# Order of the opening steps in a fused attention and feed-forward kernel: block 0's second queries and tile 0's values emitted ahead of the second key block's mixing and transposes, and one small key copy given to ScalarE

## The chip, the core and the metric

The kernel runs on one NeuronCore of one Trainium2 chip. The metric is the device time of one execution in microseconds (us), and a lower time is better. The kernel before ran five times: 209.24, 210.72, 212.59, 213.64 and 216.31 us, so the median is 212.59 us. The execution that the profile shows is the one of 209.24 us; its span from first to last instruction is 207.5 us, which leaves 1.74 us around the span.

Engines are named as in the profile: PE is TensorE (its matmuls), PEld its weight loads, DVE is VectorE, ACT is ScalarE, POOL is GpSimd, SP is the sync engine, whose queue issues DMAs. "L354" is line 354 of the kernel.

## What is computed

Attention over chunks with a memory, and then a feed-forward block with a residual. Inputs are float32; there are 4 batches, 8 heads, 768 positions, head size 64, and 8 memory keys and values per head.

```python
for c in range(S // 32):                       # chunks of 32 queries
    l, r = max(0, 32*c - 16), min(S, 32*c + 32 + 8)
    k_full = concat([mem_k, k[:, :, l:r]])     # 8 + up to 56 keys
    v_full = concat([mem_v, v[:, :, l:r]])
    a = softmax(q[:, :, 32*c:32*c+32] @ k_full.T / 8)
    out[:, :, 32*c:32*c+32] = a @ v_full
x = out with the heads side by side            # (4, 768, 512)
xn = (x - mean) / sqrt(var + 1e-6) * g_ln
result = x + relu(xn @ w_ch1) @ w_ch2          # 512 -> 2048 -> 512
```

## The kernel before

**Tiles.** A tile is 128 positions of one batch; a batch has six tiles, and three tiles make one of eight feed-forward units. Keys and queries arrive in blocks of 256 positions (two tiles). A block is first rearranged ("mixed") from the staging tile `st` or a raw float32 tile into `iv` (`mix`, L302; `mix_raw`, L268), then transposed on PE (`transpose_block`, L228; `half_q`, L290) into a PSUM bank, and copied from there into `KT` (keys: `window`, L218, with `key_piece`, L188) or `QR` (queries: `part_q`, L264). `KT` has groups of 64 positions; each holds its own keys, 16 keys to the left, 8 to the right, and the 8 memory keys. A tile reads two groups. Group 3, the second of tile 1, has as its right neighbours the first eight keys of block 1, and `first_right` (L212) copies them, four at a time, from the bank into which block 1 was transposed.

**One tile's way.** `scores` (L319, matmuls at L326) multiplies keys by queries into a pair of banks; `soften` (L335) takes the exponential on ACT, once for each half; `values` (L345: `weigh`, matmuls at L354, and `gather`, L361) multiplies by the values `V` and divides by the sum on DVE; `norm` (L374) subtracts the mean and multiplies by the gain, on DVE; `turn_x` (L395, L404, L409) transposes the result on PE and copies it; then `up_tile`, `up_two` and `up` multiply by the first weights, with a ReLU on ACT or DVE, and `down` and `paired` by the second. `v_mem` (L142) copies the memory values into `V`, two groups at a time here, on DVE. `spread_g` (L696, matmuls at L698) brings the gain vector `g_ln` onto all partitions in bank `mm[3]`; `norm(0, 0)` reads it there, and ACT copies it into `gb` for later tiles. `warm` (L591) is a matmul on zeros whose result nobody reads.

**What sets the order.** The schedule is written by hand. [...] From line 775 on, a table of steps (`at`) does the emitting for the steady part; the opening, lines 700 to 774, is a plain list of calls. The diff lies in lines 719 to 740 of that list. The DMAs of the opening are emitted before it, from line 605 to 690, and none lies among the lines of the diff.

**The queues around the diff, before.** On PE: `scores(0,0)`, eight transposes of the keys of block 1 into `mm[2]`, half of `spread_g`, the transposes of the second half of block 0's queries (into `att[1]`), `weigh(0,0)`, the other half of `spread_g`, `scores(0,1)`, four warm matmuls, `turn_x(0,0)`, `weigh(0,1)`, `up_tile(0,0,0)`. On DVE: `mix(0,1,0)`, two copies of `mix_raw`, `v_mem(0,0,2)`, `part_q`, the two copies of `first_right`, `gather(0,0)`, `norm(0,0)`, `v_mem(0,2,4)`. On ACT: `soften(0,0,0)`, `soften(0,0,1)`, four copies of `window` (pieces 2 and 3 of block 0), `soften(0,1,0)`, `soften(0,1,1)`, the copy of `gb`.

The second half of block 0's queries, which these lines transpose and copy, is what `scores(0,1)` reads; tile 0's own queries were copied before `scores(0,0)`.

Of the kernel before, what the change touches and what calls it, by code (L numbers as in the profile page):

```python
# [15 lines left out]
def kernel(  # L16
# [19 lines left out]
    W = 104  # L36
    GW = 4 * W
# [25 lines left out]
    KT = [t[:, 0 : NG * GW].rearrange("p (g j k) -> p g j k", g=NG, j=4) for t in KR]  # L63
# [20 lines left out]
    mm = [ps.tile([128, 512], FP32, name=f"mm{i}") for i in range(4)]  # L84
# [10 lines left out]
    def free(ap, off, pattern, parts=None):  # L95
        p = list(ap.ap[0]) if parts is None else [ap.ap[0][0], parts]
        return bass.AP(tensor=ap.tensor, offset=ap.offset + off, ap=[p] + [list(x) for x in pattern])

    def as16(t):
        return t.bitcast(FP16)  # L100

    def copy(eng, out, in_):
        if eng is nc.scalar:
            eng.copy(out=out, in_=in_)  # L104
        else:
            eng.tensor_copy(out=out, in_=in_)  # L106

    dve, act, pool = nc.vector, nc.scalar, nc.gpsimd
    ring = {}

    def pick(lst, key):
        key = (id(lst),) + key
        if key not in ring:
            ring[key] = ring.setdefault(("n", id(lst)), 0) % len(lst)
            ring[("n", id(lst))] += 1
        return lst[ring[key]]
# [25 lines left out]
    def v_mem(b, g0, g1, eng):  # L142
        src = memv16[96:W, b, :, :]
        copy(eng, free(V[b % 2][96:W, g0:g1, :, :], 0, [[H * VW, g1 - g0], [1, H * VW]]),
             bass.AP(tensor=src.tensor, offset=src.offset,
                     ap=[list(src.ap[0]), [0, g1 - g0], [1, H * VW]]))
# [41 lines left out]
    def key_piece(b, src, g, first, lo, n, eng, half=None):  # L188

        h, m = (0, 8) if half is None else (4 * half, 4)  # L190
        copy(eng, free(KT[b % 2], GW * g + 16 + 8 * lo + h, [[W, 4], [8, n], [1, m]]),
             free(src, 4 * (first + lo), [[1, 4], [4, n], [128, m]]))
# [16 lines left out]
            key_piece(b, banks[phase], 4 * blk + n, *PIECES[n], dve, phase)  # L209
            key_piece(b, banks[1 - phase], 4 * blk + 2 + n, *PIECES[2 + n], act, 1 - phase)  # L210

    def first_right(b, g, banks):  # L212

        for half in range(2):
            copy(dve, free(KT[b % 2], GW * g + 80 + 4 * half, [[W, 4], [1, 4]]),
                 free(banks[half], 0, [[1, 4], [128, 4]]))

    def window(b, blk, banks, k0, eng):  # L218

        for half in ((0, 1) if eng is dve else (1, 0)):  # L220
            key_piece(b, banks[half], 4 * blk + k0, *PIECES[k0], eng, half)
# [6 lines left out]
    def transpose_block(b, blk, which, banks):  # L228
        i = pick(iv, ("b", b, blk, which))
        for r in range(8):  # L230
            pv = banks[r // 4 if len(banks) == 2 else 0]
            c = 128 * (r % 4 if len(banks) == 2 else r)
            nc.tensor.matmul(  # L233
                out=pv[:, c : c + 128], lhsT=i[:, 128 * r : 128 * r + 128],
                rhs=order4 if which else identity,
                is_transpose=True, start=True, stop=True,
            )
# [26 lines left out]
    def part_q(b, blk, half, pv, eng):  # L264
        copy(eng, free(QR[b % 2], 1024 * blk + 64 * half, [[128, 8], [1, 64]]),
             free(pv, 64 * half, [[128, 8], [1, 64]]))

    def mix_raw(which, srcs, half, eng, lo=0, hi=128):  # L268

        o = pick(iv, ("b", 0, 0, which))[lo:hi, :]  # L270
        r0, n = (0, 8) if half is None else (4 * half, 4)
        for par in range(2):
            copy(eng, free(o, 128 * r0 + 64 * par, [[128, n], [1, 64]]),
                 free(srcs[par][lo:hi, :], 64 * r0, [[64, n], [1, 64]]))
# [15 lines left out]
    def half_q(b, blk, half, pv):  # L290

        i = pick(iv, ("b", b, blk, 1))
        rows = slice(64 * half, 64 * half + 64)
        for r in range(8):
            c = 128 * r + 64 * half
            nc.tensor.matmul(
                out=pv[:, c : c + 64],
                lhsT=i[rows, 128 * r : 128 * r + 128], rhs=order4[rows, rows],
                is_transpose=True, start=True, stop=True, tile_position=(64 * half, 0),
            )  # L300

    def mix(b, blk, which, eng):  # L302
        s, o = pick(st, ("b", b, blk, which)), pick(iv, ("b", b, blk, which))
        copy(eng, free(o, 0, [[64, 2], [128, 8], [1, 64]]), s)
# [14 lines left out]
    def scores(b, t):  # L319
        p = slot("att")  # L320
        score_slot[b, t] = p
        for gg in range(2):
            for j in range(4):
                for par in range(2):
                    rows = slice(64 * par, 64 * par + 64)
                    nc.tensor.matmul(  # L326
                        out=p[:, par, (4 * gg + j) * 64 : (4 * gg + j) * 64 + 64],
                        lhsT=free(KR[b % 2][rows, :], GW * (2 * t + gg) + W * j, [[1, 128]]),
                        rhs=free(QR[b % 2][rows, t // 2, :, :], 8 * gg +
                                 (32 * j + 16 * (t % 2) if (b, t) >= (1, 4) else 64 * (t % 2) + 16 * j),  # L330
                                 [[128, 8], [1, 8]]),
                        start=True, stop=True, tile_position=(64 * par, 0),
                    )

    def soften(b, t, c):  # L335
        p = score_slot[b, t]
        nc.scalar.activation(  # L337
            out=free(AT[t % 3], 32 * c, [[64, 16], [1, 32]]),
            in_=free(p, 4 * c, [[64, 16], [1, 4], [8, 8]], W),
            func=ACTF.Exp, bias=band[0:W, c : c + 1], scale=0.125,  # L340
        )
# [3 lines left out]
    def values(b, t):  # L345
        weigh(b, t)
        gather(b, t)

    def weigh(b, t):
        p = value_slot[b, t] = slot("att")  # L350
        for par in range(2):
            for j in range(4):
                for gg in range(2):
                    nc.tensor.matmul(  # L354
                        out=p[64 * gg : 64 * gg + 64, par, 128 * j : 128 * j + HD],
                        lhsT=AT[t % 3][:, par, gg, j, :],
                        rhs=V[b % 2][:, 2 * t + gg, 4 * par + j, 0:HD],
                        start=(j == 0), stop=(j == 3), tile_position=(0, 64 * gg),
                    )

    def gather(b, t):  # L361
        p, r, x = value_slot[b, t], rec[t % 2], xs[(NT * b + t) % 9]
        nc.vector.reciprocal(out=r, in_=free(p, 64, [[128, 8]]))
        nc.vector.scalar_tensor_tensor(  # L364
            out=x.rearrange("p (h d) -> p h d", h=8),
            in0=free(p, 0, [[128, 8], [1, 64]]), scalar=1.0,
            in1=free(r, 0, [[1, 8], [0, 64]]),
            op0=ALU.mult, op1=ALU.mult, accum_out=tot[t],
        )
        nc.vector.tensor_scalar(  # L370
            out=nmean[t], in0=tot[t], scalar1=-1.0 / 512, scalar2=None, op0=ALU.mult
        )

    def norm(b, t, gb=gb):  # L374
        i = NT * b + t
        nc.vector.scalar_tensor_tensor(  # L376
            out=xn[i % 4], in0=xs[i % 9], scalar=nmean[t], in1=gb, op0=ALU.add, op1=ALU.mult,
        )
# [212 lines left out]
    def warm(n, m=512, p=None):  # L591
        p = mm[3] if p is None else p
        for _ in range(n):
            nc.tensor.matmul(out=p[:, 0:m], lhsT=zero[:, 0:128], rhs=zero[:, 0:m], start=True, stop=True)
# [97 lines left out]
    K0 = [as16(mm[0]), as16(mm[1])]  # L692
    Q0 = [as16(mm[2]), as16(mm[3])]
    K1 = [as16(mm[2])[:, 512 * h : 512 * h + 512] for h in range(2)]

    def spread_g(half):  # L696
        cols = slice(256 * half, 256 * half + 256)
        nc.tensor.matmul(out=mm[3][:, cols], lhsT=gone, rhs=gpad[:, cols], start=True, stop=True)  # L698
# [20 lines left out]
    mem_vals()  # L719
    soften(0, 0, 0)  # L720
    soften(0, 0, 1)
    mix(0, 1, 0, dve)
    transpose_block(0, 1, 0, K1)
    mix_raw(1, raws[1], None, dve, 64, 128)
    spread_g(0)
    half_q(0, 0, 1, as16(att[1][:, 1, :]))
    v_mem(0, 0, 2, dve)
    part_q(0, 0, 1, as16(att[1][:, 1, :]), dve)
    first_right(0, 3, K1)
    turn["att"] = 1  # L730
    values(0, 0)
    spread_g(1)
    norm(0, 0, mm[3])
    v_mem(0, 2, 4, dve)
    window(0, 0, K0, 2, act)
    window(0, 0, K0, 3, act)
    scores(0, 1)
    soften(0, 1, 0)
    soften(0, 1, 1)
# [223 lines left out]
```

## Time and profile before

| view | value |
|---|---|
| median of five runs | 212.59 us (209.24 to 216.31) |
| the profiled execution | 209.24 us; span 207.5 us; mean granted PE clock 0.988 |
| PE busy | 198.7 us, 96% of the span |
| DVE, ACT, POOL busy | 162.6, 109.2, 109.5 us |
| DMA moved | 28.11 MB, mean 136 GB/s |
| chain that ended last, by engine | PE 75%, DVE 3%, ACT 2% |
| matmuls of the first weights, 128x384 (L430) | 464, 81.1 us |

The page divides the span into 40 equal slices of 5.19 us; a digit is the busy share in tenths, and the row PEclk gives the granted clock of PE in tenths. A line of the timeline gives the start and the duration in us, the engine, the source line, the operation, output and inputs, how many instructions were merged into the line, and in brackets how long the engine stood idle before it and what ended that. Ends of matmuls are modelled, so the distance from one group's start to the next one's is the better measure of what a group costs on PE. A row of the table by stretches gives, for each engine, the busy time and in brackets the number of instructions, then the granted clock, the DMA share and the rate.

### The profile page before, as it was taken

The page shows a single profiled execution, that of the slowest core. Times are in us where ns is not written, and L with a number is a line of the kernel's source. Part 1 is how long each engine was busy: PE and PEld are TensorE (multiplying, and loading weights), DVE is VectorE, ACT ScalarE, POOL GpSimd, SP SyncE. Part 2 cuts the span into 40 slices and gives each one's busy share as a digit, 9 for nine tenths or more (in the row PEclk, how much of TensorE's full clock was granted, in tenths as well). Part 3 has the DMA queues.
Part 4 walks back from the last instruction along what each step waited for, and adds up shares of the span by engine and source line. Part 5 has one row for each costly group of instructions (what it writes and reads, how often), then busy time and mean ns, then how long its engine had stood idle before and what let it go on. Part 6 is the DMA issues. An engine that isn't in the chain of part 4 may idle for free.

```text
span 207.5 us, 5280 instructions
## 1 busy us (share of the span) xinstructions
PE 198.7 (96%) x2042; PEld 135.4 (65%) x2042; DVE 162.6 (78%) x404; ACT 109.2 (53%) x236; POOL 109.5 (53%) x189
## 2 busy tenths in 40 slices
PE   7797999999999999999999999999999999999992
PEld 2365885547754477587667766686758765877581
DVE  5878746597989999997797999995897669565553
ACT  2575469638776076807791366537850676022300
POOL 7966687869699899954797982400040014000000
PEclk9789999999999999999999999999999999999998
DMA  5999999999999999999996999577022211220012
GB/s 161 190 187 193 206 198 187 207 129 239 166 146 141 182 194 123 154 166 249 198 166 150 128 181 125 114 164 156 17 36 76 101 30 26 78 101 0 0 54 101
DMA packets 74099, 28.11 MB, mean 136 GB/s; under 512 B 62169, under 2 KB 70105, under 8 KB 74074
## 3 DMA queue, kind: packets, MB, share of 16 engines
q0 software_dynamic: 46336, 14.71, 67.0%
q1 hardware_dynamic: 27594, 12.80, 28.0%
q8 instruction: 16, 0.26, 0.5%
q10 hardware_dynamic: 144, 0.26, 0.5%
q14 instruction: 9, 0.07, 0.1%
HBM read 30.28 MB, written 6.29 MB: 176 GB/s over the span
## 4 chain that ended last, share of the span: by engine, by line
PE 75%; DVE 3%; ACT 2%; issue 0%; DVEq 0%
PE mm L430 36%; PE mm L522 16%; PE mm L475 16%; PE att L354 3%; PE att L326 3%; ACT AT L337 1%; DVE osb L538 1%; DVE xs L364 1%; PE att L404 1%; PE att L233 0%; PE mm L233 0%; ACT rT L422 0%; ACT junk L381 0%; DVE xn L376 0%; DVE three L492 0%
## 5 line engine op out<-in xcount | busy, mean ns | idle before, releaser
L430 PE MATMUL mm<-xT,w1c 128*128 128x384 f16 x464 | 81.1, 327 | 0.0
L422 ACT ACTIVATE rT<-mm 128x384 f16<-128x384 f32 (+1 forms) x78 | 38.3, 498 | 52.7 <-PE mm L430 47.0
L430 PEld LDWEIGHTS <-w1c 128*128 128x128 f16 x464 | 51.0, 115 | 21.0
L475 PE MATMUL mm<-w2c,rT 128*128 128x512 f16 x192 | 44.4, 379 | 0.0
L137 POOL DMA_DIRECT2D V<-in_v_dram x48 | 38.4, 809 | 4.2 <-issue 2.8
L424 DVE TENSOR_SCALAR rT<-mm 128x384 f16<-128x384 f32 (+1 forms) x47 | 26.1, 559 | 14.7 <-PE mm L430 11.6
L337 ACT ACTIVATE AT<-att,band 104x512 f16<-104x512 f32 x48 | 31.0, 687 | 4.1 <-PE att L326 3.8
L387 POOL TENSOR_SCALAR veps<-sq 128x1 f32<-128x1 f32 x24 | 8.0, 334 | 43.9 <-ACT junk L381 21.9
L475 PEld LDWEIGHTS <-rT 128*128 128x128 f16 x192 | 18.2, 98 | 19.5
L381 ACT ACTIVATE junk<-xs,nmean 128x512 f16<-128x512 f32 x24 | 17.3, 720 | 4.3 <-issue 1.8
L522 PEld LDWEIGHTS <-SA 128*128 128x128 f16 x184 | 18.0, 98 | 2.1
L123 POOL DMA_DIRECT2D st<-in_q_dram x28 | 16.1, 585 | 3.6 <-DMA st<-in_q_dram 2.6
L364 DVE SCALAR_TENSOR_TENSOR xs<-att,rec 128x512 f32<-128x512 f32 x24 | 16.6, 691 | 0.8
L391 POOL TENSOR_TENSOR rstd<-veps,mhalf 128x1 f32<-128x1 f32 x24 | 16.1, 672 | 2.0
L376 DVE SCALAR_TENSOR_TENSOR xn<-xs,nmean,gb 128x512 f16<-128x512 f32 x23 | 16.6, 746 | 0.3
L522 PE MATMUL mm<-T,SA 128*128 128x256 f16 x144 | 16.7, 272 | 0.0
L522 PEld LDWEIGHTS <-rT 128*128 128x128 f16 x144 | 14.1, 98 | 3.1 <-issue 0.3
L104 ACT COPY KT<-rawk 128x352 f16<-128x352 f16 (+2 forms) x14 | 10.3, 785 | 6.5 <-DMA rawk<-iv 6.5
L129 POOL DMA_DIRECT2D st<-in_k_dram x22 | 12.9, 593 | 1.0 <-DMA w2c<-in_moe_w_ch_dram 1.0
L522 PE MATMUL mm<-w2c,rT 128*128 128x256 f16 x96 | 12.4, 272 | 0.0
L106 DVE COPY V<-memv 8x2560 f16<-8x2560 f16 (+1 forms) x14 | 11.0, 784 | 0.4
L354 PEld LDWEIGHTS <-AT 104*64 104x64 f16 x384 | 7.8, 111 | 5.3 <-issue 3.3
(107 smaller groups left out, 233.8 us busy)
## 6 DMA issues: line engine op xcount, KB each, us to landing
out_dram<-osb SPq DMA_DIRECT2D x23, 256.0 KB, 3.0
V<-in_v_dram POOLq DMA_DIRECT2D x40, 96.0 KB, 5.7
st<-in_k_dram POOLq DMA_DIRECT2D x22, 128.0 KB, 4.9
w1c<-in_moe_w_ch_dram POOLq DMA_DIRECT2D x4, 512.0 KB, 7.9
st<-in_q_dram POOLq DMA_DIRECT2D x32, 64.0 KB, 4.9
w2c<-in_moe_w_ch_dram POOLq DMA_DIRECT2D x4, 512.0 KB, 9.0
st<-in_q_dram POOLq DMA_DIRECT2D x6, 128.0 KB, 7.9
V<-in_v_dram POOLq DMA_DIRECT2D x8, 80.0 KB, 5.3
```

Of the source, the lines that this page charges most:

```text
L123: nc.gpsimd.dma_start(out=s[32 * j : 32 * j + 32, :], in_=dram(q, (b * H + j) * HS + blk * 256 * D, [[512, 32], [4 * HS, 2], [1, 512]]),)
L137: nc.gpsimd.dma_start(out=V[b % 2][lo:hi, g, :, 0:64], in_=dram(v, b * H * HS + (64 * g - 16 + lo) * D, [[64, hi - lo], [HS, H], [1, 64]]),)
L337: nc.scalar.activation(out=free(AT[t % 3], 32 * c, [[64, 16], [1, 32]]), in_=free(p, 4 * c, [[64, 16], [1, 4], [8, 8]], W), func=ACTF.Exp, ...
L364: nc.vector.scalar_tensor_tensor(out=x.rearrange("p (h d) -> p h d", h=8), in0=free(p, 0, [[128, 8], [1, 64]]), scalar=1.0, in1=free(r, 0, ...
L376: nc.vector.scalar_tensor_tensor(out=xn[i % 4], in0=xs[i % 9], scalar=nmean[t], in1=gb, op0=ALU.add, op1=ALU.mult,)
L381: nc.scalar.activation(out=junk, in_=xs[(NT * b + t) % 9], func=ACTF.Square, bias=nmean[t], scale=1.0, accum_out=sq[t],)
L391: nc.gpsimd.tensor_tensor(out=rstd[(NT * b + t) % 9], in0=veps[t % 3], in1=mhalf, op=ALU.pow)
L422: nc.scalar.activation(out=o, in_=p, func=ACTF.Relu)
L424: nc.vector.tensor_scalar(out=o, in0=p, scalar1=0.0, scalar2=None, op0=ALU.max)
L430: nc.tensor.matmul(out=p, lhsT=free(w1c[c][:, dt, :], i, [[4, 128]]), rhs=xT[u % 2][:, dt, 128 * lo : 128 * (lo + n)], start=(dt == 0), st ...
L475: nc.tensor.matmul(out=p, lhsT=rT[c][:, k_, 128 * i : 128 * i + 128], rhs=w2c[c][:, k_, :], start=(c == 0 and k_ == 0), stop=(c == 3 and k ...
L522: nc.tensor.matmul(out=p, lhsT=left(h)[:, k_, :], rhs=right(h)[:, k_, :], start=(h == 0 and k_ == 0), stop=(h == 1 and k_ == 3),)
```

## The change

Two things change. The order of the calls after `soften(0, 0, 1)` is another: `mix(0,1,0)` and the transposes of block 1's keys, which came first, come after the second half of block 0's queries; the transposes come after `values(0, 0)` as well. The `window` calls on ACT stand earlier in the list, but on ACT they still follow the same two `soften`s. One warm matmul into `mm[2]` is added between `half_q` and `values`. And `first_right` takes the engine as an argument, which is now ACT.

```diff
-    def first_right(b, g, banks):
+    def first_right(b, g, banks, eng):
 
         for half in range(2):
-            copy(dve, free(KT[b % 2], GW * g + 80 + 4 * half, [[W, 4], [1, 4]]),
+            copy(eng, free(KT[b % 2], GW * g + 80 + 4 * half, [[W, 4], [1, 4]]),
                  free(banks[half], 0, [[1, 4], [128, 4]]))
...
     mem_vals()
     soften(0, 0, 0)
     soften(0, 0, 1)
-    mix(0, 1, 0, dve)
-    transpose_block(0, 1, 0, K1)
     mix_raw(1, raws[1], None, dve, 64, 128)
     spread_g(0)
     half_q(0, 0, 1, as16(att[1][:, 1, :]))
     v_mem(0, 0, 2, dve)
+    warm(1, 512, mm[2])
     part_q(0, 0, 1, as16(att[1][:, 1, :]), dve)
-    first_right(0, 3, K1)
+    mix(0, 1, 0, dve)
     turn["att"] = 1
     values(0, 0)
+    window(0, 0, K0, 2, act)
+    window(0, 0, K0, 3, act)
+    transpose_block(0, 1, 0, K1)
+    first_right(0, 3, K1, act)
     spread_g(1)
     norm(0, 0, mm[3])
     v_mem(0, 2, 4, dve)
-    window(0, 0, K0, 2, act)
-    window(0, 0, K0, 3, act)
     scores(0, 1)
     soften(0, 1, 0)
     soften(0, 1, 1)
```

## The prediction, made before the changed kernel was run

> **What bounds the kernel now.** I read the page's first two parts, then the chain that ended last, then the timeline around the diff.
>
> ```profile
> PE 198.7 (96%) x2042; PEld 135.4 (65%) x2042; DVE 162.6 (78%) x404; ACT 109.2 (53%) x236; POOL 109.5 (53%) x189
> ...
> PEclk9789999999999999999999999999999999999998
> ```
>
> PE is nearly full, and its clock falls below full only in the opening. The chain in order of time starts at 37.80 us and is all PE from 43 us on:
>
> ```profile
> 37.80 0.70 ACT junk L381 x2
> ...
> 43.55 0.86 PE mm L475 x4
> ```
>
> So the diff, which lies between 9 and 16 us, counts only by how far it moves PE's hand-over into the full stretch. The chain doesn't reach back there; I walk it by hand in the timeline of all engines.
>
> ```profile
> 9.21 0.41 DVE L106 COPY iv<-st 128x1024 f16<-128x1024 f16 x1
> 9.66 0.49 DVE L106 CAST iv<-osb 64x512 f16<-64x512 f32 x1
> 9.77 0.61 PE L326 MATMUL att<-QR,KT 64*128 64x64 f16 x16
> 10.31 1.04 PE L233 MATMUL mm<-identity,iv 128*128 128x128 f16 x8
> 10.42 1.26 ACT L337 ACTIVATE AT<-att,band 104x512 f16<-104x512 f32 x2 [0.48 <-PE att L326]
> 11.14 0.83 PE L698 MATMUL mm<-xs,xs 128*128 128x256 f32 x2
> 11.90 0.40 PE L296 MATMUL att<-order,iv 64*128 64x64 f16 x8
> 12.23 0.44 PE L354 MATMUL att<-V,AT 104*64 104x65 f16 x16
> 12.34 0.42 DVE L106 COPY QR<-att 128x512 f16<-128x512 f16 x1 [1.19 <-PE att L296]
> 12.68 0.24 DVE L106 COPY KT<-mm 128x16 f16<-128x16 f16 x2
> 12.84 0.20 DVE L363 RECIPROCAL rec<-att 128x8 f32<-128x8 f32 x1
> 13.23 0.41 PE L326 MATMUL att<-QR,KT 64*128 64x64 f16 x16
> ```
>
> PE runs here without a gap: transposes of block 1's keys, gain, tile 1's queries, tile 0's values, tile 1's scores, each started by the one before. DVE waits 1.19 us for the queries. Then it is DVE's turn to be late:
>
> ```profile
> 14.85 0.49 DVE L106 COPY V<-memv 8x1280 f16<-8x1280 f16 x1
> 15.40 0.44 PE L354 MATMUL att<-V,AT 104*64 104x65 f16 x16
> 17.92 0.41 PE L326 MATMUL att<-QR,KT 64*128 64x64 f16 x16 [0.67 <-ACT QR L104]
> 20.04 1.08 PE L457 MATMUL mm<-xT,w1c 128*128 128x128 f16 x16 [0.52 <-DVE xT L409]
> ```
>
> Tile 1's values start at 15.40, 0.06 after the DVE copy of memory values ends (15.34), and 0.46 after the second exponential ended (13.68 + 1.26 = 14.94). So gather, norm and `v_mem(0,2,4)` on DVE set this hand-over, and ACT has 0.40 us of slack.
>
> The clock of PE by stretches:
>
> ```profile
> 8.00:9.00 1.00, 1.00 (x10) 0.56 (x9) 0.95 (x5) 0.70 (x3) 1.00 (x2) 0.54 2.17 153
> 10.00:11.00 1.00, 1.00 (x23) 0.91 (x16) 0.97 (x3) 0.58 (x1) 1.00 (x2) 0.50 1.14 190
> 11.00:12.00 1.00, 1.00 (x10) 0.67 (x8) 0.14 (x1) 1.00 (x5) 0.61 (x1) 0.76 1.18 182
> ```
>
> At half clock 0.54 means that 0.92 of that microsecond was slow, 0.76 that 0.48 was: PE ran at half speed from 8.08 to 11.48.
>
> [...] 11.48 - 8.08 = 3.40 us at 0.50. [...] scores at 17.92 wait 0.67 us for a query copy, and the warm matmuls behind them, which need nothing of it, start after, at 18.26. [...] For `first_right`'s 16 elements [...] ACT's copies into KT took 292 ns at 144 elements and 321 ns at 176, which extrapolates to 0.18. I take 0.18.
>
> **The change, part by part.** Distances between starts are used for PE.
>
> *Transposes leave the front.* They held PE from 10.31 to 11.14, 0.83 us at half clock. In their place the gain's first half starts at 10.31. Its second half, at full clock, takes 13.23 - 12.60 = 0.63; [...] So queries at 11.37, where 0.11 us of slow clock remains; the full-clock 0.33 (11.90 to 12.23) becomes 0.39: PE free at 11.76, results at about 11.83 instead of 12.30. `mix_raw` must be done: with `mix` gone from 9.21 its two copies take 9.21 to 10.03, and the raw queries, issued by 4.1 with 5.0 to landing, are there by 9.1. Cover is over a microsecond.
>
> *The added warm matmul*: 0.215, PE free at 11.97. It hides nothing else: values wait for the exponentials until 11.68 and for `v_mem` until 10.7, so it costs these 0.21 us. Values start at 11.97 instead of 12.23 and end at 12.41.
>
> *DVE*: `part_q` at 11.87 instead of 12.34 (0.47 earlier). `mix` now follows; a copy that large kept DVE 0.45 (9.21 to 9.66), and a query copy 0.34 (12.34 to 12.68): mix at 12.21, done 12.62. `first_right`, gone from here, had cost 0.16 (12.68 to 12.84). The reciprocal can start at 12.66 instead of 12.84: 0.47 - 0.45 + 0.16 = 0.18 earlier. Gather and norm behind it keep their 1.23 us: norm at 13.89 instead of 14.07, if the gain is there.
>
> *The new wait.* The transposes now wait on PE for `mix`: start 12.62 + 0.06 = 12.68, so PE stands 0.34 us (12.34 to 12.68). Queued behind: the gain's second half (norm waits for it), `scores(0,1)`, and the warm matmuls. At full clock eight transposes take 0.45 (the chain shows 0.45 for eight at 47.01). Gain at 13.13, results at 13.83, just ahead of norm's 13.89. `scores(0,1)` at 13.13 + 0.63 = 13.76 instead of 13.23: **0.53 later**. Bounds: 13.5 if mix slips in behind the queries sooner, 14.2 if half clock lasts longer.
>
> *`first_right` on ACT*: transposes end at 12.68 + 0.61 = 13.29; two copies end by 13.33 + 0.36 = 13.69. ACT is free since 12.47, the end of its `window` copies, whose place on ACT is the same. The copies are hidden under the gain's 0.63 by 0.07 us; without that cover each 0.1 us late makes scores 0.1 late.
>
> *The sum.* Exponentials 14.21 to 15.47 (1.26 us) instead of 14.94; tile 1's values at 15.47 + 0.05 = 15.52. DVE's side would be ready at 15.34 - 0.18 = 15.16. So DVE's delay is replaced by ACT's: 15.52 against 15.40, **+0.12 us**. Norm's output is turned after four warm matmuls, 13.76 + 0.34 + 0.86 = 14.96, against 14.88; its copy ends at 15.84 and `up_tile` starts at 15.97 against 15.85. ACT's queue behind (gain copy, two windows, each about 0.5 to 0.9 us) ends at 16.8, ahead of the query copy, which waits for PE (17.28 + 0.12). So scores of tile 2 and then `up_tile` at 20.04 are 0.12 later too.
>
> No DMA moves and neither SP's nor POOL's queue is touched; the second weights' third part, issued at 31.26 with 8.3 us to landing (39.6), is used at 40.34, so 0.12 us of delay costs no more there, and a gain over 0.7 us would be cut off. Profiled execution: span 207.5 + 0.12 = 207.62, time 209.24 + 0.12 = 209.36. The profiled run is the fastest of the five shown; their median is 212.59, so the forecast is **212.7 us**.
>
> **Rivals.**
>
> *The delay of `scores(0,1)` is smaller*: if it starts at 13.4, exponentials end at 15.11 and DVE's 15.16 decides: values at 15.22, 0.18 earlier than now, at most 0.3 if `mix` gains another tenth. 212.59 - 0.3 = 212.3 us. For it: PE's total work is unchanged, the transposes run at full clock. Against: `mix` sits behind `part_q`.
>
> *The clock is halved once more* (slower side). Place: PE between 14.9 and 18.3, where it is busy about 2.45 of 3.4 us, 72%, and keeps full clock; the 3.4 us ahead of the slow window were busy 1.99 us, 58%, and did not. The new wait at 12.34 and the later scores thin out PE in one of these windows. [...] 3.4 us at half clock cost 1.7: 214.4 us. Against: the new gap is 0.34 us, 10% of a window, in a stretch that was 92% busy.
>
> *Nothing moves, since another wait hides it*: PE waits for a part of the weights somewhere before 43 us, and the 0.12 is swallowed there. For it: that margin of 0.7 us; against: no wait for a DMA stands on PE in the profile. 212.6 us, not to be told from the forecast.
>
> **How the numbers follow.** Forecast, with the third rival in it (within 0.5 us of before): 0.72. Smaller delay, a gain of up to 0.3: 0.16. Clock or a longer ACT delay, 0.5 to 1.7 us slower: 0.12. All of these lie within 2%, 4.25 us, which is about what a measurement of this kernel can tell from no change. The scatter decides more than the edit: the middle three of the five runs lie from 210.72 to 213.64, and a new median may lie anywhere there. Range: 210.72 - 0.3 = 210.4 up to 213.64 + 1.7 = 215.3. That a median lies more than 2% off by scatter or a clock that I don't see I put at 0.06 faster and 0.08 slower.
>
> **What would show it.** Right: transposes (L233) after values at about 12.7 with PE idle before them for DVE's `iv`; `scores(0,1)` near 13.8; tile 1's values released by ACT's exponentials, not DVE's copy; `up_tile` near 16.0; the full stretch unchanged. Wrong: a second stretch at clock 0.5, values of tile 1 before 15.2, or PE waiting for `first_right`.

## The result, and the profile after

The change moves nothing that can be measured. Over 43 runs the changed kernel has a median of 210.17 us (208.39 to 217.8), over 80 runs beside it the kernel before has 211.5 us (208.32 to 217.85); the ratio of the times is 0.9994 with a 95% interval from 0.9974 to 1.0014. The medians lie further apart than the ratio says because they hold every execution, while the ratio leaves out those more than 1.5% above the fastest of their kernel, 13 of the 43 and 42 of the 80.

The forecast had the right direction (no change) and a level and a range that were too high: 212.7 us and 210.4 to 215.3, where 210.17 was measured. It also gave a wrong reason, which the new profile shows at once. Its execution took 210.93 us with a span of 209.1 us. First the page:

```profile
PE 198.3 (95%) x2043; PEld 134.7 (64%) x2043; DVE 163.0 (78%) x402; ACT 109.4 (52%) x238; POOL 108.3 (52%) x189
...
PEclk9999999999999999999999999999999999999999
```

This execution has no half clock in the opening (the granted clock is 1.00 in every stretch up to 45 us), so its moments can't be laid over those of before one to one. I count from the start of `scores(0,0)`, 9.77 us before and 8.78 here. The timeline of all engines:

```profile
8.78 0.41 PE L326 MATMUL att<-QR,KT 64*128 64x64 f16 x16 [0.22 <-DVE KT L106]
...
10.71 0.44 PE L354 MATMUL att<-V,AT 104*64 104x65 f16 x16
11.08 0.43 DVE L106 COPY iv<-st 128x1024 f16<-128x1024 f16 x1
...
11.56 0.62 PE L233 MATMUL mm<-identity,iv 128*128 128x128 f16 x8 [0.41 <-DVE iv L106]
...
12.22 0.25 ACT L104 COPY KT<-mm 128x16 f16<-128x16 f16 x2 [0.79 <-PE mm L233]
...
12.60 0.41 PE L326 MATMUL att<-QR,KT 64*128 64x64 f16 x16
...
13.05 1.26 ACT L337 ACTIVATE AT<-att,band 104x512 f16<-104x512 f32 x2 [0.59 <-PE att L326]
13.49 0.49 DVE L106 COPY V<-memv 8x1280 f16<-8x1280 f16 x1
...
15.24 0.19 PE L354 MATMUL att<-V,AT 104*64 104x65 f16 x1 [1.04 <-ACT KT L104]
...
15.83 0.42 PE L354 MATMUL att<-V,AT 104*64 104x65 f16 x15 [0.40 <-DMA V<-in_v_dram]
...
16.18 1.08 PE L457 MATMUL mm<-xT,w1c 128*128 128x128 f16 x16
```

The upper part is as forecast: the transposes wait 0.41 us for DVE's `mix`, the two small copies lie on ACT, and `scores(0,1)`, which stands behind the transposes on PE, comes later after `scores(0,0)` (3.82 us, not 3.46). Then comes what the forecast didn't have. The exponentials end at 14.31, DVE's copy of memory values at 13.98, and yet PE stands until 15.24, runs one matmul, and stands again until 15.83. Tile 1's values read `V` groups 2 and 3. These are the two loads of the changed kernel, with the time that they took from issue to landing (lowest, median, highest):

```profile
7.85 1.58 POOL L137 DMA_DIRECT2D V<-in_v_dram  x2
DMA to landing us min/median/max: 7.1/7.2/7.3
```

The first was issued at 7.85 and the second at about 8.64; they took 7.3 and 7.1 us, so they landed at about 15.15 and 15.75. The profile puts the first wait down to an ACT copy into `KT`, which tile 1's values don't read; the landing at 15.15 fits it, and the second wait is named as V. The same loads in the kernel before:

```profile
7.51 1.57 POOL L137 DMA_DIRECT2D V<-in_v_dram  x2
DMA to landing us min/median/max: 7.0/7.0/7.0
```

They were issued at 7.51 and 8.3, so they landed at 14.5 and 15.3. There PE started at 15.40, behind DVE's copy, which ended at 15.34: two possible releasers 0.04 us apart. The profile of before names no releaser at this row, so it can't say which of the two it was.

The two profiled spans differ by 1.6 us. 0.3 of it is there at `up_tile` (16.18 instead of 15.85), and still at 78 us (78.38 instead of 78.08 for one group of matmuls). The rest arises between 78 and 99 us, far behind the diff: there the chain now holds a transposing DMA of queries, which took 9.42 us.

```profile
82.51 9.42 DMA QR<-iv
...
93.26 0.75 DVE SA L492 x2
```

DVE waited 1.2 us for it, and PE 0.81 us for DVE after that. E6 below, in the old order, shows the same transposing DMA of 9.35 us with 0.7 us of waiting on PE, so it doesn't need the changed order.

### The profile page after: what moved, and what is told of

Its sections match the earlier page's. It is cut to its first block, busy times and chain, and to the rows that moved or that the text cites. A ratio compares the mean times of both kernels' runs of the same rounds, so it can differ in the third digit from the quotient of the medians.

```text
span 209.1 us, 5282 instructions
## 1 busy us (share of the span) xinstructions
PE 198.3 (95%) x2043; PEld 134.7 (64%) x2043; DVE 163.0 (78%) x402; ACT 109.4 (52%) x238; POOL 108.3 (52%) x189
## 4 chain that ended last, share of the span: by engine, by line
PE 67%; DVE 5%; DMA 5%; ACT 2%; issue 1%; DVEq 0%
PE mm L430 33%; PE mm L475 14%; PE mm L522 13%; DMA QR<-iv 5%; PE att L354 3%; DVE osb L538 3%; PE att L326 2%; ACT AT L337 1%; DVE xs L364 1%; PE att L404 1%; DVE three L492 0%; DVE KT L106 0%; PE att L233 0%; PE mm L233 0%; ACT rT L422 0%
## 5 line engine op out<-in xcount | busy, mean ns | idle before, releaser
L137 POOL DMA_DIRECT2D V<-in_v_dram x48 | 38.9, 819 | 5.0 <-DMA V<-in_v_dram 2.3
L387 POOL TENSOR_SCALAR veps<-sq 128x1 f32<-128x1 f32 x24 | 6.8, 284 | 43.9 <-ACT junk L381 21.9
L129 POOL DMA_DIRECT2D st<-in_k_dram x22 | 12.6, 584 | 1.7 <-DMA w2c<-in_moe_w_ch_dram 1.1
L106 DVE COPY iv<-st 128x1024 f16<-128x1024 f16 (+1 forms) x23 | 10.6, 463 | 1.5 <-DMA QR<-iv 1.2
```

Of the source, the lines that this page charges most:

```text
L137: nc.gpsimd.dma_start(out=V[b % 2][lo:hi, g, :, 0:64], in_=dram(v, b * H * HS + (64 * g - 16 + lo) * D, [[64, hi - lo], [HS, H], [1, 64]]),)
```

## The experiments

The theory after the result: the opening up to tile 1's values is closed by the landing of `V` groups 2 and 3; engines that are done earlier wait for it, whatever their order. The rival is the forecast's own reading: the queues of DVE and ACT close it.

**E1: the loads of V early, changed kernel.**

```diff
+    load_v(0, 2)
+    load_v(0, 3)
     load_w1(0)
     load_q(0, 1, 0)
-    load_v(0, 2)
-    load_v(0, 3)
     load_w1(1)
```

> The changed kernel with the loads of V groups 2 and 3 issued ahead of the first part of the first weights. Theory (the landing of V groups 2 and 3 releases tile 1's values in the changed kernel): the values of tile 1 start as soon as the exponentials are there, about 1.75 us after the start of scores(0,1), so near 14.4 us instead of 15.24 and 15.83, with no idle before them for a DMA; the first weights then land some 1.6 us later, near 15.4, and up_tile(0,0,0) starts near 15.4 instead of 16.18. Time 0.3 to 0.8 us below the changed kernel's, if nothing later takes it back. Rival (ACT's or DVE's queue releases the values, the DMA is only near): values stay at 15.2 or later, time as before.

Measured: 208.61 us (22 runs), 0.9913 of before, interval 0.9879 to 0.9947. Timeline of PE:

```profile
8.42 0.41 PE L326 MATMUL att<-QR,KT 64*128 64x64 f16 x16 [0.30 <-ACT QR L104]
...
13.58 0.44 PE L354 MATMUL att<-V,AT 104*64 104x65 f16 x16 [0.17 <-ACT AT L337]
...
13.95 1.08 PE L457 MATMUL mm<-xT,w1c 128*128 128x128 f16 x16
```

Tile 1's values now start when the exponentials are there, and `up_tile` comes 5.53 us after `scores(0,0)` instead of 7.40. The theory's reading holds. The first weights landed at about 13.9 us, 1.5 us sooner than expected, and `up_tile` did not wait for them. Between 0.9994 and 0.9913 lie 1.7 us, with some 0.8 us to either side by the two intervals; 0.3 to 0.8 us had been expected. I had cut the gain because of the margin of 0.7 us at the second weights; in this trace PE waits for no part of them.

**E2: the same loads early, kernel before.** The same edit.

> The kernel before with the same two loads moved ahead. Theory: DVE's copy of memory values stood at 15.34, 0.04 us after V group 3 landed (15.3), so without the DMA the values of tile 1 still start within 0.1 us of the end of that copy; the time is as before within 0.2 us. Rival (the DMA alone set the start in the kernel before as well): the values start up to 0.4 us earlier, when the exponentials end.

Measured: 209.16 us (22 runs), 0.9977 of before, interval 0.9943 to 1.0011. `up_tile` comes 5.87 us after `scores(0,0)`, 0.2 us less than before (6.08, with half clock in between).

```profile
13.92 0.49 DVE L106 COPY V<-memv 8x1280 f16<-8x1280 f16 x1
14.46 0.44 PE L354 MATMUL att<-V,AT 104*64 104x65 f16 x16
```

As the theory had it, tile 1's values start 0.05 us after the end of DVE's copy of memory values: with the load out of the way, DVE's queue is the last to be ready in the old order. The time can't be told from that of the kernel before.

**E3: no wait for V, changed kernel.** Tile 1's values read groups 0 and 1, so they wait neither for the loads of groups 2 and 3 nor for the second copy of memory values.

```diff
-                        rhs=V[b % 2][:, 2 * t + gg, 4 * par + j, 0:HD],
+                        rhs=V[b % 2][:, (0 if (b, t) == (0, 1) else 2 * t) + gg, 4 * par + j, 0:HD],
```

> The changed kernel in which tile 1's values read V groups 0 and 1 in place of 2 and 3, so that they wait for no load of V and for no memory value copy; tile 1's attention is then that of other values. Order and DMAs are untouched. Theory: values of tile 1 start 1.75 us after the start of scores(0,1), about 14.4 us, up_tile(0,0,0) near 14.9 instead of 16.18, 1.2 us earlier; of this 0.6 to 1.2 us reaches the end, since the third part of the second weights lands some 0.6 us before its use. Rival (ACT or DVE): values and up_tile as in the changed kernel.

Measured: 209.04 us (22 runs), 0.9906 of before, interval 0.9873 to 0.994. Values start at 14.37, `up_tile` at 14.74 (expected 14.4 and 14.9).

```profile
14.37 0.44 PE L354 MATMUL att<-V,AT 104*64 104x65 f16 x16 [0.17 <-ACT AT L337]
14.74 1.08 PE L457 MATMUL mm<-xT,w1c 128*128 128x128 f16 x16
```

No DMA was moved here, so it is this wait, not the order of loads, that is worth the time: about 1.8 us between 0.9994 and 0.9906, again with some 0.8 us to either side, where 0.6 to 1.2 had been expected. E1 moved the loads alone and the memory copy stayed where it was; the two together leave the load as the cause in the changed kernel.

**E4: more filler on PE, changed kernel.**

```diff
-    warm(4, 512, mm[1])
+    warm(8, 512, mm[1])
     turn_x(0, 0)
```

> The changed kernel with eight warm matmuls instead of four ahead of turn_x(0,0): 4 x 0.215 = 0.86 us more on PE. Theory: PE's idle 1.04 and 0.40 us before tile 1's values cover them; turn_x near 14.7 instead of 13.82, values still at the landing of V, up_tile unchanged, time unchanged within 0.1 us. Rival (no cover): up_tile and the time 0.86 us later.

Measured: 209.94 us (22 runs), 1.0007 of before, interval 0.9979 to 1.0035.

```profile
14.55 0.39 PE L404 MATMUL att<-identity,xn 128*128 128x128 f16 x4
...
15.46 0.19 PE L354 MATMUL att<-V,AT 104*64 104x65 f16 x1 [0.53 <-ACT KT L104]
...
16.01 0.41 PE L354 MATMUL att<-V,AT 104*64 104x65 f16 x15 [0.35 <-DMA V<-in_v_dram]
```

There are 0.86 us of work more on PE ahead of tile 1's values, and `up_tile` starts at 16.35 instead of 16.18: PE's idle time before the values shrank from 1.44 to 0.88 us. While a load leaves this much room, little of a reordering can show in the time.

**E5: no wait for V, kernel before.** The edit of E3.

> The kernel before in which tile 1's values read V groups 0 and 1 in place of 2 and 3, so that neither the load of V nor the second copy of memory values holds them; tile 1's attention is then that of other values. Beside the same edit of the changed kernel (0.9906 of before) this shows what the order is worth with that wait out of the way. Theory (the load of V hides the order's worth): the two differ by what the order moves, 0.2 to 0.6 us; this kernel at about 0.993 of before, up_tile(0,0,0) some 5.9 us or a little less after scores(0,0). Rival (the load of V matters in the changed kernel only, since in the kernel before DVE's chain ends later): no change, 1.000 of before.

Measured: 208.77 us (13 runs), 0.9943 of before, interval 0.9902 to 0.9984. (Here PE waited 0.7 us for a part of the second weights, the margin that I had named.) The kernel before, too, loses time to this hand-over. As the edit takes away the load and DVE's copy together, it can't say which of them; E6 can. What the order is worth without the wait was expected at 0.2 to 0.6 us. At `up_tile` nothing of it is seen: it comes 5.96 us after `scores(0,0)`, against 5.95 in E3.

```profile
13.98 0.44 PE L354 MATMUL att<-V,AT 104*64 104x65 f16 x16
14.62 1.05 PE L457 MATMUL mm<-xT,w1c 128*128 128x128 f16 x16 [0.20 <-DVE xT L409]
```

Tile 1's values start a little sooner in the old order (5.32 against 5.58 us), but then `up_tile` waits 0.20 us for DVE's copy of the turned tile. The times (0.9943 here, 0.9906 in E3, with intervals that overlap) don't exclude the 0.2 to 0.6 us.

**E6: more filler on PE, kernel before.** The edit of E4.

> The kernel before with eight warm matmuls instead of four ahead of turn_x(0,0), 0.86 us more on PE. Theory (the load of V covers it here too when the clock is full): time within 0.2 us of before. Rival (no cover in the kernel before: turn_x and the copy behind it are on the path): 0.3 to 0.5 us slower, 1.0015 to 1.0025 of before.

Measured: 211.25 us (22 runs), 1.0014 of before, interval 0.9976 to 1.0052; the time can't choose. The trace can, as its granted clock is 1.00 up to 17 us:

```profile
13.32 0.49 DVE L106 COPY V<-memv 8x1280 f16<-8x1280 f16 x1
...
13.82 0.39 PE L404 MATMUL att<-identity,xn 128*128 128x128 f16 x4
...
15.03 0.19 PE L354 MATMUL att<-V,AT 104*64 104x65 f16 x1 [0.82 <-DMA V<-in_v_dram]
...
15.57 0.41 PE L354 MATMUL att<-V,AT 104*64 104x65 f16 x15 [0.35 <-DMA V<-in_v_dram]
```

Even with the filler PE waits 1.17 us for V in the old order. DVE's copy ended at 13.81, 1.2 us ahead. This rules the rival out for the old order at full clock: it is the load that holds the values, not DVE's queue. It fits that the tie in the profile of before came from its half clock: DVE's copy ended 5.57 us after `scores(0,0)` there and 5.10 us here.

**E7: loads early, without the added warm matmul.** E1 with one line out.

```diff
     v_mem(0, 0, 2, dve)
-    warm(1, 512, mm[2])
     part_q(0, 0, 1, as16(att[1][:, 1, :]), dve)
```

> The changed kernel with the two loads of V ahead of the first weights and without the added warm matmul. Theory: in that version PE waits 0.2 us for the exponentials before tile 0's values, so the warm matmul's 0.215 us is hidden; time as with it, 0.991 of before, within 0.1 us. Rival (it delays tile 0's values): 0.2 us faster still, 0.990 of before.

Measured: 208.88 us (22 runs), 0.992 of before, interval 0.9885 to 0.9954: as E1. Values of tile 0 wait 0.55 us for the exponentials, so the warm matmul is hidden. The trace has something new:

```profile
13.75 0.44 PE L354 MATMUL att<-V,AT 104*64 104x65 f16 x16 [0.17 <-ACT AT L337]
15.76 1.08 PE L457 MATMUL mm<-xT,w1c 128*128 128x128 f16 x16 [1.56 <-DMA w1c<-in_moe_w_ch_dram]
```

The first weights, now behind V in the queue, are the next thing to be late. They took 8.2 us to landing here and 6.5 in the trace of E1, where `up_tile` didn't wait for them.

**E8: the loads of V late, kernel before.**

```diff
-    load_v(0, 2)
-    load_v(0, 3)
     load_w1(1)
+    load_v(0, 2)
+    load_v(0, 3)
```

> The kernel before with the loads of V groups 2 and 3 issued behind the second part of the first weights, about 0.8 us later. Theory (the landing of V sets the start of tile 1's values): values and up_tile(0,0,0) 0.8 to 1.5 us later, the time 0.5 to 1.5 us above before, 1.002 to 1.007. Rival (DVE's copy sets it, with a margin of 0.04 us and more when the load is quicker): below 0.3 us.

Measured: 216.81 us (6 runs), 1.0289 of before, interval 1.0226 to 1.0353. The direction is the theory's, the size is four times the upper end of what it gave.

```profile
17.34 0.19 PE L354 MATMUL att<-V,AT 104*64 104x65 f16 x1 [3.71 <-DMA V<-in_v_dram]
17.88 0.60 PE L354 MATMUL att<-V,AT 104*64 104x65 f16 x15 [0.34 <-DMA V<-in_v_dram]
```

Two terms were missed. The first of the two loads, issued at 8.33, took 8.9 us to landing instead of 7.0, so the values start 2.3 us later than in E6 (counted from `scores(0,0)`). And the clock follows: in all six executions PE's mean granted clock was between 0.957 and 0.982. The profiled one by stretches (the figure after the five engines is the granted clock):

```profile
16.00:17.00 1.00, 0.00 (x0) 0.00 (x0) 0.00 (x0) 0.00 (x0) 0.06 (x1) 1.00 2.39 152
17.00:18.00 1.00, 0.31 (x6) 0.26 (x8) 0.00 (x0) 0.00 (x0) 0.99 (x2) 0.75 1.97 181
18.00:19.00 1.00, 1.00 (x21) 0.93 (x21) 0.42 (x2) 0.00 (x0) 0.91 (x3) 0.50 1.40 208
...
24.00:25.00 1.00, 0.48 (x6) 0.22 (x4) 0.59 (x2) 0.00 (x0) 1.00 (x3) 0.84 1.23 203
```

From 17.5 to 24.3 PE runs at half clock, 6.8 us, after having stood 3.71 us. The 6.8 us are twice the 3.40 us that the slow window of the kernel before lasted. In this trace a wait for a load costs itself and, behind it, slow matmuls.

**E9 to E12**, on one chip: what is the order worth when the loads are early, and what `first_right` is worth. E9 is E1's kernel and E10 is E2's, each a second time.

> The changed kernel with the loads of V groups 2 and 3 ahead of the first weights, once more, on one chip with the next three, to measure what the order is worth with the load out of the way. Theory (the order is worth nothing even then: in the traces scores(0,0) to up_tile(0,0,0) took 5.95 us in the new order and 5.96 in the old when tile 1's values waited for no load): within 0.2% of the next kernel. Rival (the order is worth the 0.34 us of the two earlier traces, or more): 0.2% to 0.6% below it. Either way 0.990 to 0.994 of before.

> The kernel before with the same two loads moved ahead. Theory: as the new order with early loads, 0.991 to 0.994 of before. Rival: 0.2% to 0.6% above it, 0.995 to 0.999 of before.

E11 is E9 with the small copies back on DVE, E12 is E10 with the small copies alone on ACT:

```diff
 E11
-    first_right(0, 3, K1, act)
+    first_right(0, 3, K1, dve)
 E12
-    first_right(0, 3, K1)
+    first_right(0, 3, K1, act)
```

> The changed kernel with early loads of V and with first_right on DVE in place of ACT, where it stands behind the gather of tile 0. Theory (the copies must not stand behind the gather): they start about 0.5 us later than on ACT, scores(0,1) starts 4.0 instead of 3.4 us after scores(0,0) or a little less, and tile 1's values 0.4 us later; of the time at most 0.4 us, 0.002. Rival (hidden elsewhere): no difference in up_tile.

> The kernel before with early loads of V and with first_right alone given to ACT. Theory: DVE's chain (gather, norm, second copy of memory values) starts 0.16 us earlier, and since it sets tile 1's values in the old order, these and up_tile come 0.16 us earlier after scores(0,0) than in the old order with the copies on DVE (5.87 us in its trace): 5.7. In the time not to be seen. Rival: ACT's window copies behind it make tile 1's scores later, 0.2 us or more.

Measured, six runs each: E9 209.55 us, 0.9987 of before (0.9929 to 1.0046); E10 209.32 us, 0.9982 (0.9922 to 1.0042); E11 208.31 us, 0.9942 (0.9883 to 1.0001); E12 208.63 us, 0.9953 (0.9895 to 1.001). E9 and E10 can't be told apart, and both lie nearer to before than the 0.990 to 0.994 (E9) and 0.991 to 0.994 (E10) that I gave them. But the pair doesn't show that the order is worth nothing: each interval reaches 0.6% to either side, as far as the rival's upper end, and in both traces another load covers the order, as `up_tile` waits for the first weights, 1.03 us in E9 and 1.28 us in E10:

```profile
15.69 1.08 PE L457 MATMUL mm<-xT,w1c 128*128 128x128 f16 x16 [1.03 <-DMA w1c<-in_moe_w_ch_dram]
```

E11 and E12 show no such wait, and `up_tile` comes 5.89 and 5.84 us after `scores(0,0)`. On DVE the small copies start 0.5 us later than on ACT in E1 (3.56 against 3.01 us after `scores(0,0)`), half of `scores(0,1)` waits 0.18 us for them, and `up_tile` comes 0.36 us later than in E1, about as expected; in the time nothing of it can be seen. In E12 DVE's gain was expected to bring `up_tile` to 5.7 and brought 0.03 us against E2. So in the new order the engine of these copies matters to the trace, in the old order hardly, and to the time not visibly in either.

The positions in the traces, in us after the start of `scores(0,0)`:

| kernel | order | scores(0,1) | tile 1's values, first matmul | up_tile(0,0,0) | DMA that PE waited for |
|---|---|---|---|---|---|
| before (half clock to 11.48) | old | 3.46 | 5.63 | 6.08 | none named |
| after | new | 3.82 | 6.46 | 7.40 | V |
| E4 filler | new | 3.99 | 6.98 | 7.87 | V |
| E6 filler | old | 3.04 | 6.32 | 7.20 | V |
| E8 V late | old | 2.94 | 8.66 | 9.73 | V |
| E3 no wait for V | new | 3.81 | 5.58 | 5.95 | none |
| E5 no wait for V | old | 3.39 | 5.32 | 5.96 | V of tile 0 (0.26) |
| E1 V early | new | 3.39 | 5.16 | 5.53 | none |
| E2 V early | old | 3.30 | 5.42 | 5.87 | none |
| E7 V early, no warm | new | 3.40 | 5.16 | 7.17 | first weights |
| E9 V early | new | 3.71 | 5.48 | 6.95 | first weights |
| E10 V early | old | 2.93 | 5.07 | 6.80 | first weights |
| E11 V early, copies on DVE | new | 3.40 (second half 3.86) | 5.52 | 5.89 | none |
| E12 V early, copies on ACT | old | 3.26 | 5.39 | 5.84 | none |

What the order is worth once V is early stays open: up to 0.34 us at `up_tile` in favour of the new one (E1 against E2), 0.05 us against it (E11 and E12), and no difference in the time that the runs can prove.

Early loads of V are the version to try further: 0.9913 of before with 22 runs (E1), 0.9987 with six on another chip (E9, the same kernel). The first weights come late in some executions: the one profiled in E9 waited for them and took 210.07 us, the one in E1 didn't and took 208.08. How much the early loads gain is not settled, and the second measurement doesn't exclude no gain. The ratio may also understate it. Over every execution, the nine runs without the wait for V (E1 to E3, E5, E7, E9 to E12) have medians from 208.31 to 209.55 us, and the kernel before beside them 212.5 to 213.13. How that distance comes about was not tested.

## Why the prediction was right or wrong

**What bounds the kernel, the transposes, the warm matmul.** That only the hand-over into PE's full stretch counts was right, and E3 and E8 show it from both sides. (The chain is not all PE from 43 us on, as the forecast read it: at 59.47 it runs over 1.16 us of exponentials on ACT, and it ends on DVE; and PE's clock is below full in the last slice (digit 8 of the row PEclk) as well as in the opening. Nothing in the sum rests on this.) The transposes left the front and waited 0.41 us for `mix` (forecast 0.34). The forecast moved tile 0's values 0.26 us forward. That gain existed only in the half clock of the one execution: at full clock values of tile 0 start 1.93 us after `scores(0,0)` in the new order (after, E1, E3, E9; 2.08 in E4) and 1.93 to 2.03 in the old (E5, E6, E8, E10; 2.30 in E2 and 2.26 in E12). In the new order PE stands 0.2 us ahead of them for the exponentials (E1, E3, E9): what the transposes left free is spent on waiting and on the added warm matmul. (The queries at 11.37 in the forecast follow from 1.06 us for the gain's first half at half clock. That was my estimate, and no view shows it; in the kernel before the first half took 0.76 us, 0.34 of them at half clock.)

**`scores(0,1)` 0.53 us later.** Right in size. In the traces with a full clock the mean is 3.65 us in the new order (after, E1, E3, E4, E7, E9, E11) and 3.14 in the old (E2, E5, E6, E8, E10, E12), 0.51 apart. That is luck in part: single traces lie between 3.39 and 3.99 and between 2.93 and 3.39, and in E1, E7 and E11 the new order shows no wait for `mix`.

**`first_right` on ACT.** Right: a copy took 175 ns, where the forecast had taken 0.18 us from other copies; both were done at 12.47, and `scores(0,1)` at 12.60 shows no wait for them.

**"DVE's delay is replaced by ACT's", +0.12 us.** This is the step of the mechanism that failed. The row at 15.40 was read as released by DVE at 15.34, with ACT done 0.40 us ahead of it, and the search ended there. The third input of that matmul, `V`, was never given a landing time, although the view of the issues has it: 8.3 + 7.0 = 15.3. With it the forecast would have seen that in that execution no edit of the engines' order could bring the values forward by more than 0.1 us. The traces show what releases them in ACT's place: PE waited 1.44 us for V in the changed kernel, whose exponentials had ended at 14.31, 0.88 in E4 and 1.17 in E6. The rival "another wait hides it" came out nearest, but with the wrong place: I had looked for it at the second weights, at a margin of 0.7 us, and only in E5 did PE wait there.

**The clock as the slower rival.** It didn't occur in the changed kernel's profile. It did in two other traces, behind waits for a load: 6.8 us at half clock in E8, after 3.71 us of waiting, and about 3.4 us in E6, after 1.17. The busy share doesn't decide as the forecast had it. PE was busy 2.59 of the 3.40 us from 14.9 to 18.3 in the kernel before (76%, not 72%) and kept full clock; but it kept full clock in E7, too, where it was busy 1.49 of 3.40 us from 14.2 to 17.6 (44%), less than the 58% that came ahead of the slow window. When a slow stretch comes, and how long it lasts, was not shown; the forecast's 1.7 us was my estimate, half of the 3.40 us that the one in the opening of the kernel before lasted.

**The level and the range.** The number failed here. The sum gave +0.12 us, and the measured ratio is -0.06% with 0.2% to either side, about -0.13 us. But the 212.59 us to which it was added was a median of five from executions that spread over 208.32 to 217.85; 80 of them have 211.5. The step "the middle three of the five runs lie from 210.72 to 213.64, and a new median may lie anywhere there" took the spread of five numbers for the bounds of the next median, and the range began 0.2 us above the result. This term was mis-sized, and had to be widened downwards: the profiled execution, the lowest of the five, was at 209.24, and its sum of 209.36 lies 0.8 us from what was measured, the median plus the edit 2.5. Of these 2.5 us, 1.1 are the base (212.59 against 211.5). Another 1.3 are the distance between the two medians, of which the ratio shows 0.13; for that distance the forecast had no term, and its cause stays open. (The chances 0.72, 0.16 and 0.12 make 1 by themselves, so the 0.06 and 0.08 beside them can only be read as a second split.)

## What to carry to other kernels

Before a hand-over is put down to the engine that ended just ahead of it, list every input of the released instruction with its own time, loads with issue plus landing: two releasers 0.04 us apart look like one, and removing one uncovers the other. One execution also has its own course of the clock: what is tight between engines in it may have a microsecond of slack in the next (DVE's copy ended 0.04 us behind the load in the profile of before, which had half clock up to 11.48 us, and 1.2 us ahead of the values in E6, which had full clock there), so a margin should be looked for at full clock too. And where a front is closed by loads, the order of the loads is worth trying before the order of the arithmetic.

## What the runs showed of the hardware that I had not expected

- Loads of the same size took very different times to landing, by their place in POOL's queue: `V` groups 2 and 3 4.4 to 5.1 us when issued ahead of the first weights (E1, E7, E9, E10), 7.0 to 7.3 us behind the first part of them (before, after), 8.9 us behind two parts (E8). Moving a load behind one 512 KB transfer more (in the first step two loads of queries went ahead as well) made its time to landing about 2 us longer, on top of the 0.8 us or more by which it was issued later.
- The first part of the first weights took 6.2 to 6.6 us to landing in E1, E2, E11 and E12 (in the last three estimated from the end of POOL's wait for it, 14.29, 13.78 and 13.90 us, which came about 0.27 us behind the landing in E1, E7, E9 and E10) and 7.9 to 8.2 us in E7, E9 and E10, whose loads have the same order. E9 is E1's kernel and E10 is E2's, so it is not the program that decides between them; what does stays open, and it is worth 1.0 to 1.6 us of PE's idle time.
- In E8 half clock came in one stretch of 6.8 us after 3.71 us of idle PE, although PE was busy 3.00 of its first 3.40 us. In E6, after 1.17 us of waiting for V and with PE busy 1.96 of the 3.40 us ahead (58%), one stretch of about 3.4 us at half clock followed from 17.66. The changed kernel's trace has a stretch with the same 1.96 us (12.6 to 16.0) and E7's one with 1.49 us (14.2 to 17.6), and the clock stayed full behind both. So the busy share of one such stretch, counted from an arbitrary start, doesn't foretell the clock; what else decides was not measured.
